# One semaphore per chunk and bank, a query copy on another engine, and an epsilon folded into the square root, in a decode attention and SwiGLU kernel

## The chip, the cores and the metric

The kernel runs on one core of one Trainium2 chip. The metric is the device time of one execution in microseconds. The engines named below are TensorE (PE, with its weight loads as PEld), VectorE (DVE), ScalarE (ACT), GpSimd (POOL) and SyncE (SP, which issues nearly all DMAs). A row that ends in q, such as SPq, stands for the engine's sequencer, the part that reads instructions and hands them to the engine.

## The reference

One token for each of 4 batch rows is normalised, and the sum of an attention block and a feed-forward block is added to it. The attention reads a window of W = 4096 cached keys and values of each of 8 key/value heads, which 4 query heads share.

```python
xn = _layernorm(x, axis=-1)                       # x: (4, 1, 512), eps = 1e-5
# attention: 32 query heads, 8 key/value heads, Dh = 128, W = 4096
q = (xn @ wq) per head
k = k_cache[:, :, Sk - W:, :]; v = v_cache[:, :, Sk - W:, :]    # bfloat16
p = softmax(einsum(q, k) * Dh ** -0.5)
a = einsum(p, v) @ wo
# feed-forward, F = 1792
b = (silu(xn @ w_gate) * (xn @ w_up)) @ w_down
return x + a + b
```

## The kernel before

It is written by hand, engine by engine: each engine has its own program in the order of the code, and semaphores tie them. Nothing is reordered by a scheduler.

SP (`on_sync`) issues the loads on one queue: the weights for the queries, the gate and the up projection, then for each of 8 key/value heads ("groups") 4 MB of keys into one of two buffers `KB` and 4 MB of values into one of two buffers `VB`, then the down projection and the output projection `WO`, whose five pieces (`WOS`) go into the freed key buffer 0. A key load waits until the transposes of two groups earlier are done (`s_tr[15]`), a value load until the products of two groups earlier are done (`s_pv`).

Before the loop, DVE works out mean and variance of the rows (L305 to L309), ACT takes the square root (L275), DVE normalises, PE makes queries, gate and up. DVE stores the queries of all groups in `QT` and those of the first group in `QC` (L317 to L321).

PE then runs a loop of 4 rounds with two groups each (`u` = 0, 1). A group has 128 tiles of keys, handled in 16 chunks `c` of 8 tiles:

- PE transposes a chunk into PSUM (L417) and increments `s_tr[c]`; DVE (11 chunks, L328) or ACT (5 chunks, `ACT_CH`, L280) copies it to `KT`, and PE multiplies it by the queries `QC` (L432) two chunks later. Four chunks fill one PSUM bank `q` of scores.
- DVE takes maxima of each bank (L334), of all (L336), then copies the next group's queries to `QC` (L337); PE transposes the maxima (L439), DVE makes the shift `CM` (L339 to L343), PE adds it to the scores (L444, one matmul for each bank).
- ACT takes the exponentials bank by bank (L283) and PE multiplies them by the values (L453) and sums them (L459), which ends with `s_pv`.
- ACT copies the product to `Osb` (L286, `s_os`), DVE sums the denominators (L346, `s_dn`); PE picks the heads apart in the next group's chunk 2 (`fin`, L466 and L469), and DVE divides (`norm`, L350 to L355).

`spin` (L475) are matmuls without a use for their result. After the loop PE runs `fin` once more, the down projection, a permutation of the heads (L530), and the output projection (L479, L483), each piece when its `WO` load has landed. DVE and ACT copy the result (L373, L299), and ACT issues the store (L301).

A wait compares a semaphore with a number. In the loop that number depends on the round, `r * NB + (q + 1)` for `s_p` for example, since one semaphore `s_p` counts all banks of all groups, `s_ev` all chunks of DVE, `s_ea` all chunks of ACT, and `s_mk` all shifted banks. Each engine's sequencer works such a number out in a register, by an instruction of its own, ahead of the wait.

Of the kernel before, what the change touches and what calls it, by code (L numbers as in the profile page):

```python
# [10 lines left out]
def bass_parallel_sum__sliding_block_cached__swiglu_ffn__decode_kernel(  # L11
# [29 lines left out]
    NB = 4  # L41
# [35 lines left out]
    st_var = sb("st_var", [B, 1], FP32)  # L77
# [82 lines left out]
    s_ev = sem("s_ev")  # L160
    s_ea = sem("s_ea")
# [4 lines left out]
    s_mk = sem("s_mk")  # L166
    s_p = sem("s_p")
# [24 lines left out]
    def on_gpsimd(eng):  # L192
        eng.memset(ident[:], 0.0)
        eng.memset(I4[:], 0.0)
        eng.memset(ones[:], 1.0)
# [73 lines left out]
    def on_scalar(eng):  # L269
# [5 lines left out]
        eng.activation(st_std[:], st_var[:], ACT.Sqrt).then_inc(s_std, 1)  # L275

        def group(r):
            for n, c in enumerate(ACT_CH):
                eng.wait_ge(s_tr[c], r + 1)
                eng.activation(KT[:, c % 4], kt_ps[c % 3], ACT.Copy).then_inc(s_ea, 1)  # L280
            for q in range(NB):
                eng.wait_ge(s_mk, r * NB + (q + 1))
# [3 lines left out]
            eng.activation(Osb[:], O_ps, ACT.Copy).then_inc(s_os, 1)  # L286
# [3 lines left out]
        with eng.Fori(0, HKV) as r:  # L290
            group(r)
# [11 lines left out]
    def on_vector(eng):  # L303
# [3 lines left out]
        eng.bn_aggr(st_mv[:], st_bn[:])  # L307
        eng.drain()
        eng.tensor_scalar(st_var[:], st_mv[:, 1:2], EPS, None, ALU.add).then_inc(s_var, 1)  # L309
# [9 lines left out]
        eng.drain()  # L319

        eng.tensor_copy(QC[:], QT[:, 0])  # L321


        def group(n):
            for c in range(NCH):
                if c not in ACT_CH:
                    eng.wait_ge(s_tr[c], n)
                    eng.tensor_copy(KT[:, c % 4], kt_ps[c % 3]).then_inc(s_ev, 1)  # L328
# [8 lines left out]
            eng.tensor_copy(QC[:], QT[:, bass.ds(n, 1)].rearrange("p o n -> p (o n)"))  # L337
# [37 lines left out]
    def on_tensor(eng):  # L375
# [27 lines left out]
        eng.sem_inc(s_p, NB)  # L403
# [4 lines left out]
        def transposes(r, u, c):  # L408
            if c == 0:
                eng.wait_ge(d_k[u], (r - u) * 8 + 16)  # L410
            if u and c == NCH // 2:
                with eng.If(r > HKV - 2):
                    eng.wait_ge(d_kh, 16)
            if c == 2:
                eng.wait_ge(s_dn, r + 1)
# [4 lines left out]
        def scores(r, c):  # L420
            q = c * CH // BT
            if c % (NCH // NB) == 0:
                eng.wait_ge(s_p, r * NB + (q + 1))
                if q == 3:
                    eng.wait_ge(s_nrm, r + 1)
            if c in ACT_CH:
                eng.wait_ge(s_ea, r * len(ACT_CH) + (ACT_CH.index(c) + 1))
            else:
                eng.wait_ge(s_ev, r * (NCH - len(ACT_CH)) + (c + 1 - sum(a < c for a in ACT_CH)))
# [7 lines left out]
        def maxima(r):  # L437
            eng.wait_ge(s_m, r + 1)
            eng.transpose(mT_ps, m16[:], ident[:]).then_inc(s_mt, 1)  # L439

        def shift(r):
            eng.wait_ge(s_cm, r + 1)
            for q in range(NB):
                mm(ps_S[q][:].rearrange("p (t n) -> p t n", n=NH), own[:],  # L444
                   CM[:].unsqueeze(1).to_broadcast([128, BT, NH]),
                   start=False, stop=True, skip_group_check=True).then_inc(s_mk, 1)

        def pv(r, u):
            for t in range(0, NT, 2):
                n = t // 2 % 4  # L450
                if t % BT == 0:
                    eng.wait_ge(s_p, r * NB + (NB + t // BT + 1))
# [11 lines left out]
        def fin(r):  # L464
            eng.wait_ge(s_dn, r + 1)
            mm(D2_ps, head[:], dsum[:], start=True, stop=True, skip_group_check=True)  # L466
            eng.wait_ge(s_os, r + 1)
# [28 lines left out]
        def warm(r, u, n, k=2):  # L496

            if u:
                spin(n, k)
            else:  # L500
                with eng.If(r > 0):
                    spin(n, k)

        with eng.Fori(0, HKV, 2) as r0:
            for u in range(2):
                r = r0 + u
                for c in range(NCH):
                    transposes(r, u, c)
                    if c == 2:
                        fin(r)  # L510
                    if c >= 2:
                        scores(r, c - 2)
                scores(r, NCH - 2)
                scores(r, NCH - 1)
# [69 lines left out]
```

## Time and profile before

| what | value |
|---|---|
| time, median of 3 runs | 195.59 us (195.41 to 195.85) |
| profiled execution, time | 195.47 us |
| profiled execution, span from its first to its last instruction | 194.2 us |
| TensorE busy | 161.7 us, 83% of the span |
| VectorE busy | 99.7 us, 51% |
| ScalarE busy | 68.1 us, 35% |
| bytes moved by DMA | 81.17 MB, mean 418 GB/s |

The page of the profile lists the busy time of each engine, the span in 40 slices, the DMA queues, the chain of work that ended last and the costliest groups of instructions. A group of rows gives the line of the kernel, the engine, the operation, the tiles written and read, the count, the busy time, the mean duration of one, and the idle time of the engine before it with what ended it. Instructions that only set registers, branch or wait are not counted as busy; the view of one line of the source shows them, as PEldq, ACTq or DVEq.

### The profile page before, as it was taken

The page shows a single profiled execution, that of the slowest core. Times are in us where ns is not written, and L with a number is a line of the kernel's source. Part 1 is how long each engine was busy: PE and PEld are TensorE (multiplying, and loading weights), DVE is VectorE, ACT ScalarE, POOL GpSimd, SP SyncE. Part 2 cuts the span into 40 slices and gives each one's busy share as a digit, 9 for nine tenths or more (in the row PEclk, how much of TensorE's full clock was granted, in tenths as well). Part 3 has the DMA queues.
Part 4 walks back from the last instruction along what each step waited for, and adds up shares of the span by engine and source line. Part 5 has one row for each costly group of instructions (what it writes and reads, how often), then busy time and mean ns, then how long its engine had stood idle before and what let it go on. Part 6 is the DMA issues. An engine that isn't in the chain of part 4 may idle for free.

```text
span 194.2 us, 7150 instructions
## 1 busy us (share of the span) xinstructions
PE 161.7 (83%) x3179; PEld 132.8 (68%) x3179; DVE 99.7 (51%) x209; ACT 68.1 (35%) x92; POOL 5.7 (3%) x32
## 2 busy tenths in 40 slices
PE   0038972986898699999999899989996999999984
PEld 0038973985498649966994798469845984996532
DVE  0210012768177537871886389337933793688120
ACT  5520000352436242625451455315531543362520
POOL 7300000000000000000000000000000000000000
PEclk9999999999699999999999999999999999999999
DMA  6999999999999999999999999999999999999992
GB/s 216 433 437 431 423 429 432 445 429 435 425 435 442 432 422 429 425 439 432 439 432 432 432 432 432 432 439 445 432 439 439 432 398 432 466 432 392 437 407 107
DMA packets 3802, 81.17 MB, mean 418 GB/s; under 512 B 440, under 2 KB 576, under 8 KB 832
## 3 DMA queue, kind: packets, MB, share of 16 engines
q1 hardware_dynamic: 3776, 81.00, 97.3%
q8 instruction: 9, 0.15, 0.3%
q10 hardware_dynamic: 16, 0.01, 0.0%
q14 instruction: 1, 0.01, 0.0%
HBM read 81.01 MB, written 0.00 MB: 417 GB/s over the span
## 4 chain that ended last, share of the span: by engine, by line
DMA 59%; PE 34%; DVE 3%; issue 2%; SPq 1%; DVEq 0%
DMA kbuf<-in_A_k_cache_dram 43%; PE ps_kt L417 19%; DMA kbuf<-in_A_wo_dram 16%; PE ps_s L432 6%; PE ps_o L453 2%; PE ps_s L444 1%; PE ps_s L469 1%; DVE kT L328 1%; PE ps_kt L475 1%; DVE mx L334 1%; PE ps_s L483 1%; PE ps_s L466 1%; SPq L254 0%; PE ps_kt L459 0%; PE ps_kt L439 0%
## 5 line engine op out<-in xcount | busy, mean ns | idle before, releaser
L417 PE MATMUL ps_kt<-ident,kbuf 128*128 128x128 bf16 x1024 | 76.8, 221 | 10.7 <-DMA kbuf<-in_A_k_cache_dram 7.9
L417 PEld LDWEIGHTS ps_kt<-ident,kbuf 128*128 128x128 bf16 x1024 | 59.2, 98 | 13.1 <-DMA kbuf<-in_A_k_cache_dram 9.0
L328 DVE COPY kT<-ps_kt 128x1024 bf16<-128x1024 bf16 x88 | 57.6, 686 | 19.2 <-PE ps_kt L417 17.9
L280 ACT ACTIVATE kT<-ps_kt 128x1024 bf16<-128x1024 bf16 x40 | 40.9, 1023 | 53.0 <-PE ps_kt L417 53.0
L432 PE MATMUL ps_s<-qC,kT 128*128 128x16 bf16 x1024 | 44.7, 170 | 2.6 <-DVE kT L328 1.9
L432 PEld LDWEIGHTS ps_s<-qC,kT 128*128 128x128 bf16 x1024 | 37.4, 97 | 4.2 <-DVE kT L328 4.1
L283 ACT ACTIVATE p<-ps_s 128x512 bf16<-128x512 f32 x32 | 16.5, 603 | 34.0 <-PE ps_s L444 34.0
L334 DVE TENSOR_REDUCE mx<-ps_s 128x16 f32<-128x512 f32 x32 | 22.0, 689 | 5.9 <-PE ps_s L432 3.8
L475 PE MATMUL ps_kt<-own,ones 128*128 128x512 bf16 x82 | 20.7, 380 | 0.0
L453 PE MATMUL ps_o<-vbuf,p 128*32 128x256 bf16 x512 | 18.6, 284 | 0.3
L453 PEld LDWEIGHTS ps_o<-vbuf,p 128*32 128x32 bf16 x512 | 14.6, 100 | 6.0 <-ACT p L283 4.6
L346 DVE TENSOR_REDUCE dsum<-ps_kt 128x16 f32<-128x256 f32 x8 | 3.4, 425 | 28.6 <-PE ps_kt L459 28.6
L459 PE MATMUL ps_kt<-p,ones 128*32 128x256 bf16 x64 | 16.4, 282 | 0.0
L475 PEld LDWEIGHTS ps_kt<-own,ones 128*128 128x128 bf16 x82 | 6.6, 97 | 7.0 <-issue 1.1
L444 PE MATMUL ps_s<-cm,own 128*128 128x512 bf16 x32 | 8.9, 402 | 1.0 <-DVE cm L343 1.0
L380 PE MATMUL ps_s<-i,xn 4*128 4x4 f32 x4 | 0.6, 255 | 10.3 <-DVE xn L313 10.3
L380 PEld LDWEIGHTS ps_s<-i,xn 4*128 4x128 f32 x4 | 0.6, 208 | 10.3 <-issue 10.3
L459 PEld LDWEIGHTS ps_kt<-p,ones 128*32 128x32 bf16 x64 | 6.5, 101 | 0.1
L289 ACT ACTIVATE ex<-ps_o 128x84 f32<-128x84 f32 x1 | 0.2, 240 | 17.4 <-PE ps_o L399 17.4
L444 PEld LDWEIGHTS ps_s<-cm,own 128*128 128x128 bf16 x32 | 2.5, 99 | 5.5 <-DVE cm L343 3.4
L286 ACT ACTIVATE osb<-ps_o 128x256 f32<-128x256 f32 x8 | 3.1, 383 | 8.2 <-PE ps_kt L459 8.2
L359 DVE TENSOR_SCALAR ex<-ex 128x84 f32<-128x84 f32 x1 | 0.2, 204 | 10.9 <-ACT ex L289 10.9
(83 smaller groups left out, 89.8 us busy)
## 6 DMA issues: line engine op xcount, KB each, us to landing
vbuf<-in_A_v_cache_dram SPq DMA_DIRECT2D x8, 4096.0 KB, 30.2
kbuf<-in_A_k_cache_dram SPq DMA_DIRECT2D x7, 4096.0 KB, 26.7
vbuf<-in_A_wq_dram SPq DMA_DIRECT2D x1, 4096.0 KB, 12.4
kbuf<-in_A_k_cache_dram SPq DMA_DIRECT2D x2, 2048.0 KB, 25.4
kbuf<-in_A_wo_dram SPq DMA_DIRECT2D x1, 2048.0 KB, 27.2
wg_sb<-in_B_w_gate_dram SPq DMA_DIRECT2D x1, 1792.0 KB, 16.2
wu_sb<-in_B_w_up_dram SPq DMA_DIRECT2D x1, 1792.0 KB, 21.1
wd_sb<-in_B_w_down_dram SPq DMA_DIRECT2D x1, 1664.0 KB
```

The costliest lines, as they stand in the source:

```text
L280: eng.activation(KT[:, c % 4], kt_ps[c % 3], ACT.Copy).then_inc(s_ea, 1)
L283: eng.activation(P[:, BT * q:BT * (q + 1), :], ps_S[q][:].rearrange("p (t n) -> p t n", n=NH), ACT.Exp, scale=SCALE).then_inc(s_p, 1)
L286: eng.activation(Osb[:], O_ps, ACT.Copy).then_inc(s_os, 1)
L328: eng.tensor_copy(KT[:, c % 4], kt_ps[c % 3]).then_inc(s_ev, 1)
L334: eng.tensor_reduce(mx[:, q, :], ps_S[q][:].rearrange("p (t n) -> p n t", n=NH), AX.X, ALU.max)
L346: eng.tensor_reduce(dsum[:], den_ps.rearrange("p (t n) -> p n t", n=NH), AX.X, ALU.add).then_inc(s_dn, 1)
L417: last = eng.transpose(kt_ps[c % 3][:, k, :], KB[u][:, CH * c + k, :], ident[:])
L432: last = mm(ps_S[q][:, NH * t:NH * (t + 1)], KT[:, c % 4, k, :], QC[:], start=(t == 0), stop=False, skip_group_check=True)
L444: mm(ps_S[q][:].rearrange("p (t n) -> p t n", n=NH), own[:], CM[:].unsqueeze(1).to_broadcast([128, BT, NH]), start=False, stop=True, skip_ ...
L453: mm(O_ps[32 * n:32 * n + 32, :], P[:, t:t + 2, :].rearrange("p t n -> p (t n)"), VB[u][:, t:t + 2, :].rearrange("p t d -> p (t d)"), star ...
L459: last = mm(den_ps[32 * n:32 * n + 32, :], ones[:, 0:32], P[:, DT * e:DT * (e + 1), :].rearrange("p t n -> p (t n)"), start=(e < 4), stop= ...
L475: mm(ps_kt[k][:], ones[:], own[:].unsqueeze(1).to_broadcast([128, 4, 128]), skip_group_check=True)
```

## The change

Three things are changed.

1. The semaphores `s_ev` and `s_ea` become 16 semaphores `s_ev[c]`, one for each chunk; `s_mk` and `s_p` become four each, one for each bank. Each is incremented once in a group, so that every wait in the loop compares with the loop's own counter, which now runs from 1. PE works out three numbers in a round with `snap` (`d` for the loads, `n`, `n1`), and no other.
2. The copy of the next group's queries to `QC` moves from DVE (after the maxima) to ACT (after the copy to `Osb`); `s_os` is incremented by it, and no longer by the copy to `Osb`. The first group's queries are copied to `QC` by DVE from PSUM, where before they were copied from `QT` after a drain.
3. The addition of epsilon on DVE, and the drain ahead of it, go; ACT's square root adds epsilon as its bias, read from a small tile `st_eps` that POOL fills.

```diff
-    s_ev = sem("s_ev")
-    s_ea = sem("s_ea")
+    s_ev = [sem("s_ev%d" % i) for i in range(NCH)]
-    s_mk = sem("s_mk")
-    s_p = sem("s_p")
+    s_mk = [sem("s_mk%d" % i) for i in range(NB)]
+    s_p = [sem("s_p%d" % i) for i in range(NB)]
...
         eng.memset(I4[:], 0.0)
+        eng.memset(st_eps[:], EPS)
...
-        eng.activation(st_std[:], st_var[:], ACT.Sqrt).then_inc(s_std, 1)
+        eng.activation(st_std[:], st_mv[:, 1:2], ACT.Sqrt, bias=st_eps[:, 0:1]).then_inc(s_std, 1)
...
             for q in range(NB):
-                eng.wait_ge(s_mk, r * NB + (q + 1))
+                eng.wait_ge(s_mk[q], n)
                 eng.activation(P[:, BT * q:BT * (q + 1), :], ps_S[q][:].rearrange("p (t n) -> p t n", n=NH),
-                               ACT.Exp, scale=SCALE).then_inc(s_p, 1)
-            eng.wait_ge(s_pv, r + 1)
-            eng.activation(Osb[:], O_ps, ACT.Copy).then_inc(s_os, 1)
+                               ACT.Exp, scale=SCALE).then_inc(s_p[q], 1)
+            eng.wait_ge(s_pv, n)
+            eng.activation(Osb[:], O_ps, ACT.Copy)
+            eng.activation(QC[:], QT[:, bass.ds(n, 1)].rearrange("p o n -> p (o n)"), ACT.Copy).then_inc(s_os, 1)
...
-        eng.bn_aggr(st_mv[:], st_bn[:])
-        eng.drain()
-        eng.tensor_scalar(st_var[:], st_mv[:, 1:2], EPS, None, ALU.add).then_inc(s_var, 1)
+        eng.bn_aggr(st_mv[:], st_bn[:]).then_inc(s_var, 1)
...
-        eng.drain()
-
-        eng.tensor_copy(QC[:], QT[:, 0])
+        eng.tensor_copy(QC[:].rearrange("p (b h) -> p b h", b=B),
+                        q_ps.rearrange("p (k h b) -> p k b h", k=HKV, b=B)[:, 0])
...
             eng.tensor_reduce(m16[:], mx[:].rearrange("p q n -> p n q"), AX.X, ALU.max).then_inc(s_m, 1)
-            eng.tensor_copy(QC[:], QT[:, bass.ds(n, 1)].rearrange("p o n -> p (o n)"))
             eng.wait_ge(s_mt, n)
...
-        def scores(r, c):
+        def scores(c, n):
             q = c * CH // BT
             if c % (NCH // NB) == 0:
-                eng.wait_ge(s_p, r * NB + (q + 1))
+                eng.wait_ge(s_p[q], n)
                 if q == 3:
-                    eng.wait_ge(s_nrm, r + 1)
-            if c in ACT_CH:
-                eng.wait_ge(s_ea, r * len(ACT_CH) + (ACT_CH.index(c) + 1))
-            else:
-                eng.wait_ge(s_ev, r * (NCH - len(ACT_CH)) + (c + 1 - sum(a < c for a in ACT_CH)))
+                    eng.wait_ge(s_nrm, n)
+            eng.wait_ge(s_ev[c], n)
...
-                    eng.wait_ge(s_p, r * NB + (NB + t // BT + 1))
+                    eng.wait_ge(s_p[t // BT], n1)
...
-        with eng.Fori(0, HKV, 2) as r0:
+        with eng.Fori(1, HKV + 1, 2) as m:
+
+            d = eng.snap((m - 1) * 8 + 16)
             for u in range(2):
-                r = r0 + u
+                n = m if u == 0 else eng.snap(m + 1)
+                n1 = eng.snap(n + 1)
```

The first place is TensorE's program in the loop, chunks 6 and 7 of a group's transposes with the scores of chunks 4 and 5 (`qC` and `kT` are the queries and the copied chunk). Before:

```order
L417 MATMUL ps_kt<-ident,kbuf 128x128 x8
L423 REGISTER_ALU
L429 REGISTER_ALU [waits s_p]
L432 MATMUL ps_s<-qC,kT 128x16 [waits s_ev]
L432 MATMUL ps_s<-qC,kT 128x16 x7
L417 MATMUL ps_kt<-ident,kbuf 128x128 x8
L427 REGISTER_ALU
L432 MATMUL ps_s<-qC,kT 128x16 [waits s_ea]
L432 MATMUL ps_s<-qC,kT 128x16 x7
```

The same place with the change:

```order
L415 MATMUL ps_kt<-ident,kbuf 128x128 x8
L427 MATMUL ps_s<-qC,kT 128x16 [waits s_ev4,s_p1]
L427 MATMUL ps_s<-qC,kT 128x16 x7
L415 MATMUL ps_kt<-ident,kbuf 128x128 x8
L427 MATMUL ps_s<-qC,kT 128x16 [waits s_ev5]
L427 MATMUL ps_s<-qC,kT 128x16 x7
```

The instructions that work out a number are gone; the matmuls stand as they stood. TensorE's whole program has 249 such rows before and 201 with the change.

The second place is ScalarE's program from its last chunk copy to the end. The piece of the difference, with the rows of before marked - and those of the change marked +:

```order
-L282 ISA
-L283 ACTIVATE p<-ps_s 128x512 [waits s_mk]
-L282 REGISTER_ALU
-L283 ACTIVATE p<-ps_s 128x512 [waits s_mk]
-L282 REGISTER_ALU
...
 L286 ACTIVATE osb<-ps_o 128x256 [waits s_pv]
-L290 REGISTER_ALU
-L290 COMPARE_AND_BRANCH
...
+L287 ISA
+L287 ACTIVATE qC<-qT 128x16
+L291 REGISTER_ALU
+L291 COMPARE_AND_BRANCH
```

The numbers for `s_mk` go, and one instruction for the address of the queries and the copy to `qC` come in behind the copy to `osb`. ScalarE's program has 32 rows before and 29 with the change.

The third place is VectorE's program from the maxima of the last bank to the end of the loop and the first rows behind it. Before:

```order
L334 TENSOR_REDUCE mx<-ps_s 128x16 [waits s_sc3]
L336 TENSOR_REDUCE m<-mx 128x16
L337 REGISTER_ALU
L337 COPY qC<-qT 128x16
L339 TENSOR_TENSOR junk<-ps_kt,moff 16x128 [waits s_mt]
...
L346 TENSOR_REDUCE dsum<-ps_kt 128x16 [waits s_pv]
L366 REGISTER_ALU
L366 COMPARE_AND_BRANCH
L350 RECIPROCAL den<-ps_s 128x16 [waits s_fin]
```

With the change:

```order
L332 TENSOR_REDUCE mx<-ps_s 128x16 [waits s_sc3]
L334 TENSOR_REDUCE m<-mx 128x16
L336 TENSOR_TENSOR junk<-ps_kt,moff 16x128 [waits s_mt]
...
L343 TENSOR_REDUCE dsum<-ps_kt 128x16 [waits s_pv]
L363 REGISTER_ALU
L363 COMPARE_AND_BRANCH
L347 RECIPROCAL den<-ps_s 128x16 [waits s_fin]
```

Two instructions leave the loop. VectorE's program has 46 such rows before and 43 with the change, and the diff takes two drains besides, which these rows do not show: five instructions fewer in all. SyncE's program is the same in both; GpSimd's has one more, the fill of `st_eps`.

More of the change, by code (lines that the diff above doesn't have):

```diff
@@ L402, in on_tensor @@
         last.then_inc(s_gu, 1)
[L403 removed]
+        for q in range(NB):
+            eng.sem_inc(s_p[q], 1)
         eng.sem_inc(s_dn, 1)
```

82 lines of the change are left out of this document (41 added, 41 removed).

## The prediction

> **What bounds the kernel now.** I read the page first, for the share of each engine, the DMA queues and the chain that ended last.
>
> ```profile
> span 194.2 us, 7150 instructions
> ...
> PE 161.7 (83%) x3179; PEld 132.8 (68%) x3179; DVE 99.7 (51%) x209; ACT 68.1 (35%) x92; POOL 5.7 (3%) x32
> ...
> POOL 7300000000000000000000000000000000000000
> ...
> q1 hardware_dynamic: 3776, 81.00, 97.3%
> q8 instruction: 9, 0.15, 0.3%
> q14 instruction: 1, 0.01, 0.0%
> ...
> DMA 59%; PE 34%; DVE 3%; issue 2%; SPq 1%; DVEq 0%
> ```
>
> No engine is full, but SP's queue q1 keeps the 16 DMA engines busy for 97.3% of the span. The DMA view for the stretch from 78 to 189 us tells whether anything is lost there.
>
> ```profile
> q1 hardware_dynamic: 2170, 47.76, 99.9%
> ```
>
> Nothing is: for 111 us the data queue alone takes 99.9% of the engines. So the loads are a stream that does not break, and only its start and its end can move the time. The waits and the chain of waits show how TensorE stands to it.
>
> ```profile
> PEld ps_kt L417 <- DMA kbuf<-in_A_k_cache_dram: 9.0, 4, 4.6
> SPq L241 <- PE ps_kt L417: 71.8, 5, 28.3
> SPq L267 <- DMA out_dram<-y_sb: 32.3, 1, 32.3
> 159.24 0.34 SPq L254
> 160.09 31.06 DMA kbuf<-in_A_wo_dram
> 191.20 1.23 PE ps_s L483 x16
> 192.44 0.41 DVE y_sb L373
> ```
>
> TensorE waits for keys four times, 9.0 us in all, so it is ahead of the stream. SP does wait for TensorE (71.8 us), but only to queue loads behind others: the output projection is issued at 159.24 and lands some 31 us later, because that much is queued before it. The chain ends with these loads, 1.2 us of matmuls, a copy and the store. The timeline from 183.65 us shows how close TensorE runs behind the stream there.
>
> ```profile
> 183.65 0.38 ACT L286 ACTIVATE osb<-ps_o 128x256 f32<-128x256 f32 x1 [0.83 <-PE ps_kt L459]
> 184.34 0.53 PEld L469 LDWEIGHTS ps_s<-sel,osb 128*128 128x128 f32 x4
> 185.01 0.26 DVE L350 RECIPROCAL den<-ps_s 128x16 f32<-128x16 f32 x1 [0.93 <-PE ps_s L469]
> 186.18 0.45 ACT L294 ACTIVATE oP<-ps_kt 128x64 bf16<-128x64 f32 x1 [2.14 <-PE ps_kt L530]
> 191.20 1.21 PE L483 MATMUL ps_s<-kbuf,oP 128*4 128x256 bf16 x16 [0.63 <-DMA kbuf<-in_A_wo_dram]
> 191.81 0.09 PEld L483 LDWEIGHTS ps_s<-kbuf,oP 128*4 128x4 bf16 x4 [0.20 <-DMA kbuf<-in_A_wo_dram]
> 192.12 0.08 PEld L483 LDWEIGHTS ps_s<-kbuf,oP 128*4 128x4 bf16 x2 [0.22 <-DMA kbuf<-in_A_wo_dram]
> ```
>
> TensorE had done all it could at 190.57 (191.20 less 0.63), waited for the third piece of `WO`, and waited again for the two behind it, for the last till 192.12. Its lead is 0.63 us. Last comes the DMA view for 189.6 to 193 us, whose row gives the rate in 40 slices of 0.085 us.
>
> ```profile
> GB/s 229 386 253 193 350 301 265 289 277 253 349 241 277 229 241 217 145 96 24 24 24 24 24 24 0 0 0 0 0 0 0 0 0 0 0 0 0 0 0 0
> ```
>
> All 16 engines together moved about 430 GB/s (47.76 MB in 111 us), so one moves 27. The six slices at 24, from 191.13 to 191.64, are one engine working alone for 0.5 us while fifteen have nothing left. TensorE's last weight load starts 0.48 us behind its end. That lone engine is what ends the kernel.
>
> Why is it late? The view for 189 to 190 us has one packet that is not data:
>
> ```profile
> q14 instruction: 1, 0.01, 1.9%
> ```
>
> It is 8 KB of an engine's program, and it held one DMA engine for 1.9% of 16 us, 0.30 us, in the last 2 us of the stream. That it held the very engine that is late is an inference from the place and the size (0.30 us in service, and the turn of the data behind it); no view names the engine of a packet.
>
> **The change part by part.** First the registers, by the views of their lines:
>
> ```profile
> L429 PEldq ALU_OP  x80: 32/32/36, 35.9 to 177.0; - x80
> L423 PEldq ALU_OP  x24: 32/32/32, 38.1 to 175.2; - x24
> L427 PEldq ALU_OP  x32: 32/32/32, 38.6 to 175.8; - x32
> L452 PEldq ALU_OP  x32: 32/32/36, 49.3 to 182.5; - x32
> L282 ACTq ALU_OP  x24: 35/35/44, 49.7 to 181.2; - x24
> ```
>
> On TensorE 168 of 32 ns, less the 8 of L452 that stay, are 160 x 32 ns = 5.1 us of its sequencer, 0.64 us in each of 8 groups. Between zero (the sequencer runs ahead of the matmuls) and 0.64 us a group I take about zero for the time, at either end: what TensorE gains in a group it loses at the next wait for keys (9.0 us in four waits), and a lead at the end that grows from 0.63 us does not bring the loads. Without that cover it would be 5.1 us. On ScalarE 24 x 35 ns stand between exponentials and go the same way. The waits themselves stay, and what is queued behind each stays too.
>
> The copy of the queries, by the views of the lines that are nearest in kind:
>
> ```profile
> L337 DVE COPY qC<-qT x8: 159/161/164, 47.9 to 178.9; 128x16 bf16 x8
> L275 ACT ACTIVATE st_std<-st_var x1: 202/202/202, 9.2 to 9.2; 4x1 f32<-4x1 f32 x1
> L289 ACT ACTIVATE ex<-ps_o 128x84 f32<-128x84 f32 x1 | 0.2, 240 | 17.4 <-PE ps_o L399 17.4
> DVE junk L339 <- PE ps_kt L439: 1.9, 8, 0.2
> ```
>
> VectorE loses 161 ns behind the maxima; there it waits for the transposed maxima anyway (L339, 1.9 us over 8 times), so nothing is gained. ScalarE gains one of 161 to 240 ns; I take 0.2, since the smallest activation of this trace is 202. Behind it waits `s_os`, and behind that TensorE's `fin`. In the loop 24 transposes stand ahead of `fin`; the weakest cover is the last `fin`: `Osb` ends at 184.03 (183.65 + 0.38), the copy then at 184.23 to 184.27, and L469 loads at 184.34. The margin is 0.1 us; if handing over costs more than that, the excess, at most 0.2 us by these rows, comes off TensorE's lead of 0.63. Cost zero. The next chunk that ScalarE copies is `c` = 3 of the next group, behind `fin`, so it is not held.
>
> Epsilon and the first queries, by one row and one wait:
>
> ```profile
> L309 DVE TENSOR_SCALAR st_var<-st_mv x1: 142/142/142, 9.0 to 9.0; 4x1 f32<-4x1 f32 x1
> PE ps_s L387 <- DMA vbuf<-in_A_wq_dram: 2.4, 1, 2.4
> ```
>
> VectorE saves 142 ns and two drains; a bias on the square root costs ScalarE between nothing and its own 202 ns again. TensorE waits 2.4 us for the query weights afterwards, so either sign is covered: zero. The fill of `st_eps` delays the load of `x` by one more small memset, under the same 2.4 us.
>
> By instructions, then, the sum is zero. What is left is the code itself. The packet on q14 comes when five engines' programs are at their ends: SP has stood in its last wait for 32.3 us, GpSimd's row in the page is empty after its second slice, TensorE's code comes on q8; VectorE and ScalarE have just left their loops (L350 at 185.01, L294 at 186.18) and read code that they have not read before. One of the two crosses the end of a block of its program there. VectorE's program becomes five instructions shorter and ScalarE's a few, ahead of that place, so the crossing moves that far towards the end or behind it, and the packet may be asked for only when the loads are done. Then the lone engine ends with the others: 0.5 us earlier, at 191.13 in place of 191.64, and the last piece is seen at 191.6 in place of 192.12. TensorE is free by then: from 190.57, its 16 matmuls take 1.21 us less two waits, about 0.8, until 191.4. The gain is 0.5 us; its bounds are 0 (the packet stays, or hit another engine) and 1.0 us (the last 0.40 MB spread evenly over all engines):
>
> ```profile
> DMA packets 263, 0.40 MB, mean 118 GB/s; under 512 B 40, under 2 KB 147, under 8 KB 263
> ```
>
> 0.40 MB at 430 GB/s are 0.93 us from 189.6, so the loads would end at 190.5 and TensorE's own 191.4 would decide, in place of 192.41 (191.20 + 1.21).
>
> The Trainium skill speaks against this term: its page "Runtime: NRT & Kernel Launch", section "Instruction fetch mechanics", has the sequencer fetch the next block while it executes the current one and calls the cost of a crossing mostly hidden. By that the sum is zero, 195.6 us. It names 16 KiB blocks; q8's 9 packets of 0.15 MB agree, q14's 8 KB does not. The same section has a taken branch outside a window of two blocks fetch again; TensorE's loop branches back three times, and the row for 78 to 189 us lists no q8 packet, so here it does not.
>
> The profiled execution took 195.47 us, 1.3 more than its span and 0.12 less than the median of 195.59. Less 0.5 it is 194.97, as a median 195.1.
>
> **The rivals.** *Nothing that lasts* (195.6 us). The packet is still asked for before 189 us, because the block ends earlier in the program than I think, or ScalarE's, where only few instructions go, is the one; or the late engine was another. For it: every instruction term is zero. A measurement of this kernel tells about 0.2%, 0.4 us, from no change.
>
> *A block of code lands worse* (slower). The row for 76 to 78 us is one TensorE block:
>
> ```profile
> q8 instruction: 1, 0.02, 2.9%
> ```
>
> It holds one DMA engine for 2.9% of 32 us, 0.93 us. TensorE's blocks are now cut at other instructions. If one more falls to an engine that is already late, that engine ends 0.9 us later still: 195.6 + 0.9 = 196.5 us. It decides as soon as the engine ends over 0.4 us behind 191.64. Against it: TensorE's program gets shorter, so there should be no more blocks.
>
> *ScalarE's copy holds the end* (slower). The price is 0.2 us of `fin`, and it decides only beyond the lead of 0.63 us: 195.6 unless TensorE also loses 0.8 us somewhere, then 196.0.
>
> *TensorE's registers are on the path* (faster): 195.6 - 5.1 = 190.5 us. The 99.9% row excludes it, since no byte less is moved.
>
> **How the numbers follow.** Lone engine gone: 0.50, 195.1 us, by itself 194.8 to 195.3. Nothing that lasts: 0.38, 195.4 to 195.8. A block lands worse: 0.08. ScalarE's copy: 0.03. Registers: 0.01. The range of 194.8 to 195.8 holds the first two and leaves out 0.12. Faster by over 0.2%: the first and the last, 0.51; within: 0.38; slower: 0.11.
>
> **What would show it.** Right: no q14 packet in the last us of the stream, no slices at the rate of one engine at its end, no idle time of 0.6 us before L483, and a span about 0.5 us shorter with q1 still at 97%. Also TensorE waiting longer for keys, VectorE's L339 as before, and L469 where it was. Wrong: the lone engine is there without a q14 packet, or the packet is there and no engine is late; or a q1 share that falls below 97%, which would mean that something starves the stream.

## The result, and the profile after

The changed kernel takes 195.18 us (median of 13 runs, 195.01 to 195.38) against 195.67 us for the kernel before, measured beside it (13 runs, 195.41 to 196.46). The ratio is 0.997, with a 95% interval of 0.9959 to 0.9981: 0.49 us faster by the medians. Forecast were 195.1 us and a gain of 0.5 us.

The page of the changed kernel, the rows that answer to those of before:

```profile
span 193.9 us, 6951 instructions
...
PE 163.8 (84%) x3179; PEld 135.2 (70%) x3179; DVE 99.0 (51%) x200; ACT 69.1 (36%) x100; POOL 5.7 (3%) x33
...
q1 hardware_dynamic: 3776, 81.00, 97.5%
q8 instruction: 8, 0.13, 0.2%
q10 hardware_dynamic: 16, 0.01, 0.0%
...
PE 48%; DMA 44%; DVE 5%; issue 1%; SPq 1%; ACT 0%; DVEq 0%
```

There are 199 instructions fewer (7150 less 6951), and SP's loads fill 97.5% of the engines' time, 97.3% before: the bound is the same. The row of q14 is missing. The ninth packet of q8 is gone too, but that says nothing: before, it came at 193.4 us, behind the loads, and two variants below whose TensorE program is as long as the one of before also show eight. The chain now has more of TensorE (48%, was 34%) and less of DMA (44%, was 59%); the rows of the end tell why. First the DMA view of the changed kernel for 189.6 to 193 us, 40 slices of 0.085 us:

```profile
GB/s 277 277 386 193 289 277 301 265 325 265 289 277 289 265 277 205 121 72 48 24 24 24 12 0 0 0 0 0 0 0 0 0 0 0 0 0 0 0 0 0
DMA packets 255, 0.41 MB, mean 120 GB/s; under 512 B 38, under 2 KB 138, under 8 KB 255
```

Six slices at the rate of one engine have become three and a half, some 0.3 us in place of 0.5. Then the timeline of the changed kernel, from ScalarE's copies to the end:

```profile
184.16 0.38 ACT L286 ACTIVATE osb<-ps_o 128x256 f32<-128x256 f32 x1 [0.84 <-PE ps_kt L454]
184.44 0.21 ACT L287 ACTIVATE qC<-qT 128x16 bf16 x1
...
184.86 0.53 PEld L464 LDWEIGHTS ps_s<-sel,osb 128*128 128x128 f32 x4
...
189.61 0.60 PE L478 MATMUL ps_s<-s,sel 128*4 128x256 f32 x4 [0.70 <-ACT s L298]
...
190.04 2.08 PE L478 MATMUL ps_s<-kbuf,oP 128*4 128x256 bf16 x32
191.51 0.09 PEld L478 LDWEIGHTS ps_s<-kbuf,oP 128*4 128x4 bf16 x4 [0.18 <-DMA kbuf<-in_A_wo_dram]
191.85 0.08 PEld L478 LDWEIGHTS ps_s<-kbuf,oP 128*4 128x4 bf16 x2 [0.25 <-DMA kbuf<-in_A_wo_dram]
...
192.17 0.41 DVE L370 CAST y_sb<-ps_s 4x256 bf16<-4x256 f32 x1 [5.04 <-PE ps_s L478]
```

L478 is before's L483. Its matmuls of 32 tiles now run in one stretch of 2.08 us from 190.04: the wait of 0.63 us for the third piece of `WO` is gone. The copy of the queries (L287) takes 0.21 us, and the weight load of `fin` (L464) follows the end of `Osb` by 0.32 us (184.86 less 184.54), before by 0.31 (184.34 less 184.03): at the end of the kernel the copy costs nothing. The last piece is seen at 191.85, 0.27 us earlier than in the profile before.

So this profile shows only 0.3 us. Two things account for it. The profiled executions lie on opposite sides of their medians, 195.30 us against 195.18 with the change and 195.47 against 195.67 before. And TensorE was itself later here: the matmuls of `s` (189.61) began 0.52 us later than before:

```profile
189.09 0.60 PE L483 MATMUL ps_s<-s,sel 128*4 128x256 f32 x4 [0.70 <-ACT s L297]
```

The lead of 0.63 us was used up. That is why the chain now runs back through TensorE instead of stopping at the load of `WO`.

Whether TensorE gained in its groups by the numbers it no longer works out is seen at the first transposes of the last two groups. The chain of waits of the changed kernel has the first of them and its timeline the second:

```profile
149.01 1.51 PE ps_kt L415 x24
```

```profile
166.44 0.73 PE L415 MATMUL ps_kt<-ident,kbuf 128*128 128x128 bf16 x10
```

The group between them takes 17.43 us. The same two views of the kernel before:

```profile
148.65 1.51 PE ps_kt L417 x24
```

```profile
166.00 0.79 PE L417 MATMUL ps_kt<-ident,kbuf 128*128 128x128 bf16 x11
```

There it is 17.35 us. This group did not get shorter, and it began 0.36 us later, when its keys had landed. The waits of the changed kernel, for keys and for the transposed maxima:

```profile
PEld ps_kt L415 <- DMA kbuf<-in_A_k_cache_dram: 9.6, 4, 4.6
DVE junk L336 <- PE ps_kt L434: 2.5, 8, 0.3
```

TensorE waits 9.6 us for keys, again four times, where it was 9.0: of the 5.1 us that 160 numbers less could spare it, little is seen here, and that is waited away. (By the trace it is 168 rows ALU_OP and 24 FUSED_REGOPS less, some 6.3 us, with 27 instructions on semaphores more; the prediction's sum left out the FUSED_REGOPS.) VectorE's wait (L336, before L339) rose from 1.9 to 2.5 us: part of the 1.3 us of the eight copies that left it (8 x 161 ns) is now waiting.

### The profile page after: what moved, and what is told of

Its sections match the earlier page's. It is cut to its first block, busy times and chain, and to the rows that moved or that the text cites. A ratio compares the mean times of both kernels' runs of the same rounds, so it can differ in the third digit from the quotient of the medians.

```text
span 193.9 us, 6951 instructions
## 1 busy us (share of the span) xinstructions
PE 163.8 (84%) x3179; PEld 135.2 (70%) x3179; DVE 99.0 (51%) x200; ACT 69.1 (36%) x100; POOL 5.7 (3%) x33
## 3 DMA queue, kind: packets, MB, share of 16 engines
q1 hardware_dynamic: 3776, 81.00, 97.5%
## 4 chain that ended last, share of the span: by engine, by line
PE 48%; DMA 44%; DVE 5%; issue 1%; SPq 1%; ACT 0%; DVEq 0%
DMA kbuf<-in_A_k_cache_dram 44%; PE ps_kt L415 23%; PE ps_s L427 8%; PE ps_o L448 5%; PE ps_kt L470 4%; DVE kT L326 2%; PE ps_s L439 2%; PE ps_s L464 2%; DVE mx L332 2%; PE ps_s L478 1%; PE ps_s L474 1%; PE ps_s L461 1%; PE ps_kt L454 1%; PE ps_kt L434 0%; ACT s L298 0%
## 5 line engine op out<-in xcount | busy, mean ns | idle before, releaser
L415 PE MATMUL ps_kt<-ident,kbuf 128*128 128x128 bf16 x1024 | 78.2, 224 | 9.0 <-DMA kbuf<-in_A_k_cache_dram 8.5
L415 PEld LDWEIGHTS ps_kt<-ident,kbuf 128*128 128x128 bf16 x1024 | 60.6, 100 | 11.2 <-DMA kbuf<-in_A_k_cache_dram 9.6
L427 PEld LDWEIGHTS ps_s<-qC,kT 128*128 128x128 bf16 x1024 | 38.4, 97 | 4.6 <-DVE kT L326 4.1
L448 PE MATMUL ps_o<-vbuf,p 128*32 128x256 bf16 x512 | 19.1, 289 | 0.3
L454 PE MATMUL ps_kt<-p,ones 128*32 128x256 bf16 x64 | 16.9, 287 | 0.0
L439 PE MATMUL ps_s<-cm,own 128*128 128x512 bf16 x32 | 8.3, 380 | 1.0 <-DVE cm L340 1.0
L464 PE MATMUL ps_s<-sel,osb 128*128 128x16 f32 x36 | 5.8, 275 | 0.0
```

Of the source, the lines that this page charges most:

```text
L415: last = eng.transpose(kt_ps[c % 3][:, k, :], KB[u][:, CH * c + k, :], ident[:])
L427: last = mm(ps_S[q][:, NH * t:NH * (t + 1)], KT[:, c % 4, k, :], QC[:], start=(t == 0), stop=False, skip_group_check=True)
L439: mm(ps_S[q][:].rearrange("p (t n) -> p t n", n=NH), own[:], CM[:].unsqueeze(1).to_broadcast([128, BT, NH]), start=False, stop=True, skip_ ...
L448: mm(O_ps[32 * n:32 * n + 32, :], P[:, t:t + 2, :].rearrange("p t n -> p (t n)"), VB[u][:, t:t + 2, :].rearrange("p t d -> p (t d)"), star ...
L454: last = mm(den_ps[32 * n:32 * n + 32, :], ones[:, 0:32], P[:, DT * e:DT * (e + 1), :].rearrange("p t n -> p (t n)"), start=(e < 4), stop= ...
L464: last = mm(O2_ps, Osb[:, Dh * h:Dh * (h + 1)], sel[:, NH * h:NH * (h + 1)], start=(h == 0), stop=(h == 1), skip_group_check=True)
```

## The experiments

A word that recurs: the **length** of an engine's program, that is every instruction that it holds, waits and drains too. Before, VectorE has 64, ScalarE 35 and TensorE 2256; with the change 59, 33 and 2217. A drain is an instruction without work of its own, which I use to make a program longer.

**The two halves of the change.** The first keeps the new semaphores and undoes the rest (VectorE again 64 long, ScalarE 31):

```diff
-        eng.activation(st_std[:], st_mv[:, 1:2], ACT.Sqrt, bias=st_eps[:, 0:1]).then_inc(s_std, 1)
+        eng.activation(st_std[:], st_var[:], ACT.Sqrt).then_inc(s_std, 1)
...
-            eng.activation(Osb[:], O_ps, ACT.Copy)
-            eng.activation(QC[:], QT[:, bass.ds(n, 1)].rearrange("p o n -> p (o n)"), ACT.Copy).then_inc(s_os, 1)
+            eng.activation(Osb[:], O_ps, ACT.Copy).then_inc(s_os, 1)
...
+            eng.tensor_copy(QC[:], QT[:, bass.ds(n, 1)].rearrange("p o n -> p (o n)"))
```

> The semaphores alone: the query copy and the epsilon are as before, so VectorE's program has all of its instructions again (64, the change has 59), TensorE's is short (2217 for 2256) and ScalarE's shorter than both (31 for 35). Theory: the block of VectorE's program is what the end of the loads waits for, so the q14 packet is back in the last 2 us of the loads and the time is that of before, 195.6 us. Rival, ScalarE's block: no packet, 195.2. Rival, TensorE's registers and waits: 195.2, packet or not.

Measured: 195.56 us (195.42 to 195.82), ratio 0.9981 (0.9965 to 0.9998); the kernel before took 195.73 beside it. Its DMA view for 189 to 190 us has the packet,

```profile
q14 instruction: 1, 0.01, 1.9%
```

and from 189.6 us, in slices of 0.085 us:

```profile
GB/s 361 277 434 60 458 193 301 193 325 265 265 277 253 349 241 277 205 217 157 96 36 24 24 24 24 24 24 0 0 0 0 0 0 0 0 0 0 0 0 0
```

The packet and six slices of a lone engine are back. Its waits for keys:

```profile
PEld ps_kt L417 <- DMA kbuf<-in_A_k_cache_dram: 12.3, 6, 4.7
```

They are 3.3 us longer than before, and 0.6 us in the changed kernel's profile: some of what TensorE is spared it waits, and none of it brings the loads.

The second half is the kernel before with the copy on ScalarE and epsilon as the bias, and the old semaphores (VectorE 59, ScalarE 37, TensorE 2256):

```diff
-        eng.activation(st_std[:], st_var[:], ACT.Sqrt).then_inc(s_std, 1)
+        eng.activation(st_std[:], st_mv[:, 1:2], ACT.Sqrt, bias=st_eps[:, 0:1]).then_inc(s_std, 1)
...
-            eng.activation(Osb[:], O_ps, ACT.Copy).then_inc(s_os, 1)
+            eng.activation(Osb[:], O_ps, ACT.Copy)
+            eng.activation(QC[:], QT[:, bass.ds(r + 1, 1)].rearrange("p o n -> p (o n)"), ACT.Copy).then_inc(s_os, 1)
...
-            eng.tensor_copy(QC[:], QT[:, bass.ds(n, 1)].rearrange("p o n -> p (o n)"))
```

> The other half: the query copy on ScalarE and the epsilon as bias, with the semaphores and register sums of before. VectorE's program is as short as with the change (59), TensorE's as long as before (2256), ScalarE's longer than both (37). Theory: no q14 packet, 195.2 us. Rival, ScalarE's block: the packet is there and the time 195.6. Rival, TensorE's registers and waits: 195.6 without a packet.

Measured: 195.22 us (195.12 to 195.76), ratio 0.9971 (0.9956 to 0.9985). Its DMA view for 189.6 to 193 us:

```profile
GB/s 410 265 422 169 374 181 337 265 265 289 337 289 265 277 301 241 169 157 84 48 24 0 0 0 0 0 0 0 0 0 0 0 0 0 0 0 0 0 0 0
```

and the last piece in its timeline:

```profile
191.71 0.08 PEld L481 LDWEIGHTS ps_s<-kbuf,oP 128*4 128x4 bf16 x2 [0.24 <-DMA kbuf<-in_A_wo_dram]
```

No q14 packet, one slice of a lone engine, and the last piece at 191.71, where the profile before has 192.12. So this half alone brings 0.51 us, as much as the whole change. The register instructions that the first half saves bring at most the 0.2 us between it and the kernel before, and the spans below say that they bring nothing.

**The packet alone.** The changed kernel, with drains on VectorE ahead of its loop and nothing else. Five make VectorE 64 long again, three make it 62:

```diff
+        for _ in range(5):
+            eng.drain()
```

> The whole change, with five empty drains on VectorE ahead of its loop, which make its program as long as before (64) and do nothing else. Theory: the q14 packet is back and the time is 195.6 us. Both rivals: 195.2 and no packet.

Measured with five: 195.59 us (195.28 to 195.82), ratio 0.9981 (0.9966 to 0.9996). Its DMA view for 189 to 190 us has

```profile
q14 instruction: 1, 0.01, 1.9%
```

and from 189.6 us, in slices of 0.085 us:

```profile
GB/s 253 325 289 145 530 96 362 217 241 313 265 265 289 253 265 265 229 193 72 72 36 24 24 24 24 24 0 0 0 0 0 0 0 0 0 0 0 0 0 0
```

Five useless instructions, which VectorE passes before its loop, take 0.41 of the 0.49 us away again (195.59 less 195.18, measured at different times), and the packet and the lone engine are back.

> The whole change, with three empty drains on VectorE ahead of its loop in place of five: 62 instructions, between the change's 59 and the 64 of before. It narrows down where the block ends. Theory: either the packet is in the last 2 us of the loads and the time is 195.6 us, or it is not and the time is 195.2; nothing between.

Measured with three: 194.95 us (194.86 to 195.09), ratio 0.9955 (0.9938 to 0.9971); the kernel before took 195.62 beside it. Its DMA view for 194 to 195 us, behind the end of the span at 193.7, has the packet, at 194.55 us:

```profile
q14 instruction: 1, 0.01, 1.9%
```

The view from 189.6 us shows no lone engine but for half a slice:

```profile
GB/s 313 458 253 398 181 362 301 241 325 289 277 301 265 253 253 181 145 84 72 48 12 0 0 0 0 0 0 0 0 0 0 0 0 0 0 0 0 0 0 0
```

Three drains cost nothing, two more cost 0.64 us (by medians measured at different times). It is not the drains' time, but the length of the program: between 62 and 64 instructions VectorE asks for another block while the loads still run.

**Late or only there?** If the packet costs because it comes late, then asking for it early should cost nothing. The kernel before, with 14 drains on VectorE ahead of its loop (length 78), so that the end of the block falls into the loop:

```diff
+        for _ in range(14):
+            eng.drain()
```

> The kernel before, with 14 empty drains on VectorE ahead of its loop, so that the place at which the block is asked for moves from behind the loop into it and is passed in the first round. Theory: the q14 packet comes before 60 us; what it costs there is open: 195.2 us if its DMA engine is one that has time to spare at the end, 195.6 or more if it is one that is late anyway. Both rivals: the packet stays at the end, 195.6.

Measured: 195.56 us (195.34 to 195.99), ratio 0.9975 (0.9957 to 0.9993). Its DMA view for 53 to 54 us has the packet, at 53.5 us,

```profile
q14 instruction: 1, 0.01, 1.9%
```

and yet the end, from 189.6 us, looks like this:

```profile
GB/s 386 313 241 361 205 277 265 277 325 289 373 253 289 265 277 265 253 193 133 72 36 24 24 24 12 0 0 0 0 0 0 0 0 0 0 0 0 0 0 0
```

The lone engine stays for 0.3 us, no more than in the changed kernel's profile; but this profiled execution, 195.35 us, is the second fastest of its twelve, and the median is 0.34 us above that of the second half of the change, measured beside it (195.22). So the early block costs about as much as the late one. The expectation had left that open.

**What the spans say.** Each run also has its span, from the first to the last instruction of the program. It leaves out the 1.2 to 1.5 us of the time that most runs have outside of it, and it separates the kernels better than the time does:

| kernel | VectorE's length | its further block at | span, median of the runs | time less span, median |
|---|---|---|---|---|
| before (94 runs beside the variants) | 64 | 189.3 us | 194.3 us | 1.27 to 1.30 us |
| new semaphores alone | 64 | 189.5 us | 194.3 us | 1.26 us |
| change and 5 drains | 64 | 189.6 us | 194.3 us | 1.26 us |
| before and 14 drains | 78 | 53.5 us | 194.3 us | 1.24 us |
| change and 3 drains | 62 | 194.55 us | 193.7 us | 1.25 us |
| query copy and epsilon alone | 59 | none | 193.8 us | 1.41 us |
| the change | 59 | none | 193.8 us | 1.39 us |

VectorE's block costs 0.5 to 0.6 us of the span, early or late, and the register instructions cost nothing of it. The last column holds something that nobody forecast: the kernels whose VectorE program has 59 instructions take some 0.1 us more outside of the span. That is 0.14 of the 0.23 us by which the kernel with three drains (194.95 us) is faster than the change (195.18); why it is so, no run shows. The kernel before has runs that are long outside of the span, 10 of the 35 beside the two halves by 0.4 us and more, and they raise its median there (195.73 us).

**What the single packets say.** The trace keeps the start, duration and size of every packet. In the kernel before, data packets of one size take the same time after 40 us, within 20 ns (196 ns for 5 KB, 309 ns for 8 KB, 1213 ns for 32 KB), but for those that begin just as a packet of a program ends, and in one place the one behind it as well. These are the data packets behind the blocks of VectorE and ScalarE (whose runs follow below):

| block | took | data packets behind it | in place of | lost by that DMA engine |
|---|---|---|---|---|
| VectorE, late (before, 189.3 us) | 309 ns | 504 and 429 ns (5 KB) | 196 ns each | 0.85 us |
| VectorE, early (14 drains, 53.5 us) | 309 ns | 1744 ns (32 KB) | 1213 ns | 0.84 us |
| ScalarE, late (33 drains, 187.76 us) | 309 ns | 551 ns (8 KB) | 309 ns | 0.55 us |
| ScalarE, early (36 drains, 59.5 us) | 309 ns | 1453 ns (32 KB) | 1213 ns | 0.55 us |

So a block costs its DMA engine more than its own 0.31 us, because the data behind it are held up too. With the new semaphores alone and with 5 drains the packets behind VectorE's block take 504 and 429, and 501 and 429 ns, and from there one follows the other without a gap to the very last packet of the stream: the lone engine is the one that served the block. Why the data are held up, and why more behind VectorE's block than behind ScalarE's, no run shows.

**The other engine.** ScalarE's program made longer in the changed kernel, by 31, 33 and 36 drains (length 64, 66 and 69):

```diff
+        for _ in range(31):   # 33, 36
+            eng.drain()
```

> The whole change, with 31 empty drains on ScalarE ahead of its loop, which bring its program from 33 instructions to 64, the length at which VectorE's asks for its next block; VectorE's stays at 59. Theory: a block is a block, so a q14 packet comes again, now for ScalarE, and if ScalarE crosses the same place behind its loop, it comes in the last us of the loads and the time is 195.6 us. Rival, only VectorE's program matters: no packet, 195.2.

> The whole change, with 33 empty drains on ScalarE ahead of its loop. With 31 its block was asked for after its 64th and last instruction, the store; with 36, in the loop. So the place is the 65th instruction, and with 33 that is the copy of the result behind the loop, which ScalarE's sequencer reads at about 184 us. Theory, the place of the crossing in time is what costs, whoever crosses: the q14 packet comes between 185 and 191.5 us and the time is 195.6 us. Rival, only VectorE's blocks cost: 195.2.

> The whole change, with 36 empty drains on ScalarE ahead of its loop in place of 31 (its program has 69 instructions, VectorE's 59). With 31 the q14 packet came at 193.7 us, when ScalarE issued its last instruction, the store, and cost nothing. Five more put the same place in the program ahead of the store, behind the loop. Theory, the place of the crossing in time is what costs: the q14 packet comes between 184 and 191.5 us and the time is 195.6 us. Rival, only VectorE's blocks cost: 195.2.

Measured:

| drains | length | packet at | median (range) | ratio (95%) | before, beside it |
|---|---|---|---|---|---|
| 31 | 64 | 193.66 us | 195.12 (194.96 to 195.42) | 0.9974 (0.9962 to 0.9987) | 195.60 |
| 33 | 66 | 187.76 us | 195.37 (195.26 to 195.52) | 0.9976 (0.9965 to 0.9988) | 195.75 |
| 36 | 69 | 59.5 us | 195.30 (195.09 to 195.68) | 0.9973 (0.9956 to 0.9990) | 195.62 |

With 31 the packet comes, as expected, but behind the store, and costs nothing; 195.6 us was expected. With 36 it was meant for the end and fell into the loop, so that run says only what an early packet costs. With 33 it came in the last 4 us of the stream, and the loss that I expected did not follow. That kernel's DMA view for 187 to 188 us has

```profile
q14 instruction: 1, 0.01, 1.9%
```

and from 189.6 us, in slices of 0.085 us:

```profile
GB/s 410 410 205 374 253 301 169 301 289 265 362 289 301 277 241 229 205 145 97 36 24 12 0 0 0 0 0 0 0 0 0 0 0 0 0 0 0 0 0 0
```

The same packet with the same 0.30 us of service, and one slice and a half of a lone engine. Against the run with 31 drains it is 0.25 us, against the changed kernel 0.19, and the ratios to the kernel before do not differ. The medians of the spans are 193.7, 194.0 and 193.9 us for 31, 33 and 36 drains: ScalarE's block costs 0.1 to 0.3 us, VectorE's 0.5 to 0.6. The table of the packets has the reason for most of that: ScalarE's takes 0.55 us from its DMA engine, VectorE's 0.85, and some 0.3 us of either go unnoticed. With 33 drains, too, the data behind the block run without a gap to the last packet of the stream.

**How bad a TensorE block is.** First try: 256 increments of an unused semaphore at TensorE's start, to shift where its blocks end.

```diff
+        s_pad = sem("s_pad")
+        for _ in range(256):
+            eng.sem_inc(s_pad, 1)
```

> The whole change, with 256 increments of an unused semaphore at the start of TensorE's program, where it waits 10 us for the normalised rows anyway: one q8 block of 16 KB more (9 in place of 8) while the loads run. This prices the rival of the prediction in which one more block falls to an engine. If the ninth block falls to an engine that has none, it costs nothing that lasts beyond the others: 195.2 us. If it falls to one that is late anyway: 0.9 us or more on top, 196.1 or more.

Measured: 215.41 us (212.72 to 215.59), ratio 1.101 (1.0993 to 1.1027). This tests nothing of what it was made for, as three views of that kernel show. Its timeline has TensorE's first matmul at 40 us,

```profile
40.37 0.61 PE L380 MATMUL ps_s<-i,xn 4*128 4x4 f32 x4 [40.37 <-issue]
```

its waits have SP's queue behind TensorE's first results,

```profile
SPq L251 <- PE ps_s L387: 40.7, 1, 40.7
```

and its page has the data queue:

```profile
q1 hardware_dynamic: 3776, 81.00, 89.5%
```

TensorE started at 40 us, since 256 increments held it until then, 0.16 us each. SP waited for its first results before it could issue a load of values into the buffer of the query weights, the stream broke, and q1 fell to 89.5%. It does show the other side of the bound: the gap in the stream was not made good, and the kernel takes 20 us longer.

The second try puts 62 small matmuls without use ahead of TensorE's loop, which moves its blocks without delaying anything that the loads need:

```diff
+        for _ in range(62):
+            mm(ps_kt[2][:, 0:NH], ones[:], own[:, 0:NH], skip_group_check=True)
```

> The whole change, with 62 small matmuls without use on TensorE ahead of its loop, where it waits about 5 us for the first keys. They cost 62 x 23 ns = 1.4 us there and lengthen its program by 124 instructions, so that TensorE crosses the end of one of its own blocks behind the loop and not at the very end: a ninth q8 packet of 16 KB comes between 185 and 191 us. It prices the prediction's rival of a block that lands worse. Theory: it holds a DMA engine for 0.93 us and the data behind it longer; 195.2 us if that engine is one that is done early, up to 196.6 if it is late anyway. Rival, small matmuls and no block: 195.2 with the packet missing.

Measured: 196.58 us (196.40 to 196.98), ratio 1.004 (1.0023 to 1.0057). Its DMA view for 190 to 192 us has a block of TensorE's program,

```profile
q8 instruction: 1, 0.02, 3.0%
```

the view from 189.6 us the end of the stream,

```profile
GB/s 217 434 229 398 241 265 253 410 289 253 337 253 265 241 205 133 145 109 109 48 0 24 0 24 0 0 24 24 24 24 24 24 24 24 24 0 0 0 0 0
```

and the timeline TensorE's wait:

```profile
192.26 1.05 PE L480 MATMUL ps_s<-kbuf,oP 128*4 128x256 bf16 x16 [1.42 <-DMA kbuf<-in_A_wo_dram]
```

The block comes at 190.2 us. For the last 15 slices, 1.3 us, at most one engine moves data, and TensorE stands idle for 1.42 us. It costs 1.4 us against the changed kernel, 1.3 us by the spans (195.1 against 193.8). By the single packets the block took 0.97 us, and the four data packets behind it 227, 225, 225 and 132 ns in place of 84: some 1.4 us lost by one DMA engine, whose packets then run without a gap to the last of the stream.

**An attempt to beat both.** If single engines are what ends the kernel, the last loads should lie on more of them. The rows of the down projection `WDX` go out by two DMAs of 8 partitions in place of four of 4:

```diff
-        for o in range(4):
-            eng.dma_start(WDX[o:JX:4], wdx_ap[o]).then_inc(d_wd, 16)
+        for o in range(2):
+            eng.dma_start(WDX[o:JX:2], wdx_ap[o]).then_inc(d_wd, 16)
```

> The whole change, with the small rest of the down projection (16 partitions) loaded by two DMAs of 8 partitions in place of four of 4, so that by the Trainium skill's page on DMA it runs on 8 engines in place of 4, with half as much on each. If the late block of code falls among the four engines, their load is why it cannot be absorbed; here, without a late block, the time should stay at 195.2 us, and rise towards 195.8 if the second four engines are ones that blocks of TensorE's code made late.

Measured: 196.36 us (196.26 to 196.40), ratio 1.004 (1.0027 to 1.0054), 1.2 us above the changed kernel, where 195.2 to 195.8 was expected. Its end, from 189.6 us:

```profile
GB/s 542 265 374 373 386 470 398 422 373 446 374 349 470 277 289 325 229 277 145 169 253 169 181 181 193 193 121 108 72 48 36 24 24 24 0 0 0 0 0 0
```

From about 191.1 to 191.8 us the rate is 145 to 253 GB/s, that of some 5 to 9 engines: now several have too much left. But most of the loss is older. At 189.6 us this kernel still has 0.73 MB to load and the changed one 0.41, and up to 180 us both had loaded some 76.7 MB. Between 180 and 185 us the small rows of `WDX` are loaded, by the order of the issues (the 4.2 MB of `WO` follow them). The DMA view of that stretch with two DMAs of 8 partitions, and then of the changed kernel:

```profile
q1 hardware_dynamic: 143, 1.84, 100.4%
```

```profile
q1 hardware_dynamic: 172, 2.18, 101.9%
```

The engines are as busy and move 0.34 MB less, 0.8 us at 430 GB/s. That is where two thirds of the 1.2 us are lost; why less is moved there stays open.

On top of that, the last large piece of `WO` by 16 DMAs of 8 partitions each, to spread it in another way:

```diff
-        for q in range(len(WOS) - 1):
+        for q in range(len(WOS) - 2):
...
+        for p in range(0, 128, 8):
+            eng.dma_start(WO[p:p + 8, WOS[-2]:NR, :], wo_ap[p:p + 8, WOS[-2]:NR, :]).then_inc(d_wo[-1], 16)
```

> As the kernel with two DMAs, and the last piece of the output projection, 128 KB, loaded by 16 DMAs of 8 partitions, so that it runs on the first 8 engines alone and the other 8 have 8 KB less each, 0.3 us at 27 GB/s. If TensorE's code blocks made just the other 8 late, the loads end 0.3 us earlier and the time is 194.9 us, faster than both kernels. If they are mixed among the first 8, these end 0.3 us later: 195.5.

Measured: 199.60 us (199.46 to 199.76), ratio 1.0208 (1.0194 to 1.0222). The timeline:

```profile
161.28 18.02 SPq L268 DMA_DIRECT2D kbuf<-in_A_wo_dram  x16
...
195.98 0.38 PE L480 MATMUL ps_s<-kbuf,oP 128*4 128x256 bf16 x2 [2.79 <-DMA kbuf<-in_A_wo_dram]
```

SP needed 18 us to issue the sixteen, 1.1 us each, and TensorE waited 2.79 us for the last, until 195.98 us. The DMA view shows no data behind 193.4 us, so this wait is not for bytes, and the slow issue was over at 179.3; what it is stays open. Expected were 194.9 or 195.5 us. Neither is a better kernel.

## Why the prediction was right

**The stream bounds, and instructions sum to zero: shown.** The first half of the change takes 160 and more register instructions off TensorE, 5.1 us of its sequencer by the prediction's count, and the span stays at 194.3 us. The rival that would have given 190.5 us is out. The other terms taken at nothing are at nothing: the copy on ScalarE takes 207 ns where 0.2 us was put down, and `fin` follows `Osb` as before (0.32 us, before 0.31), so the margin of 0.1 us that was named as the weakest cover held. (The smallest activation of the trace is 199 ns, not 202; nothing hangs on it.)

**The packet on q14 and the 0.5 us: shown.** The program block of 8 KB at 189.3 us, VectorE's, is what the change removes. It comes and goes with two instructions, and the span with it: 194.3 us in the four kernels that have it while the loads run, 193.7 to 193.8 in the three that do not. The prediction inferred that the block held the engine that is late; the single packets of the two kernels that bring it back show that engine, and that it loses 0.31 us to the block and 0.54 to the slower data behind it. The prediction put down the first part as a number and the second only in words ("the turn of the data behind it").

**What was off, and what was luck.** Of the signs that were named, no q14 packet, the missing wait of 0.63 us and q1 at 97% came. Others did not: slices at the rate of one engine are still there (three and a half), VectorE's wait at L339 rose from 1.9 to 2.5 us, and the first weight load of `fin` came 0.52 us later. A lone engine without a q14 packet was even named as a sign of being wrong. It is not that here, because the span goes with the block in seven kernels, but it shows that the block is not all that makes an engine late: the loads ended at 191.3 to 191.6 us without VectorE's block, not at 191.13. The prediction did not say whether VectorE or ScalarE asks for the block; it is VectorE. It put the last piece at 191.6 in the profile, and it was 191.85, since it took TensorE to be free from 190.57, and in this execution TensorE worked until 191.4 without a wait for loads. The lead of 0.63 us is no fixed quantity: in the profiles with the block the same wait is 0.63, 0.54, 0.46 and 0.30 us. Its wording, that the crossing moves "behind" the loads, made lateness the point, and that is too narrow, since VectorE's block at 53 us costs as much as at 189 us. And that the time gained 0.49 us, so near to 0.5, is in part luck: the span gained 0.5 us, but the change added some 0.1 us outside of the span that the prediction did not have. By these two it would be 0.4 us, near the lower end of the interval of the ratio (0.37 to 0.80 us).

**The slower rival was real, but another kernel's.** A block that lands worse was priced at 0.9 us, from the 0.93 us of a TensorE block, on top of 195.6: 196.5 us. Forced by 62 matmuls it gave 196.58, but that is agreement by chance: the kernel with the matmuls has no block of VectorE's, so the step is 1.4 us from 195.18, half as much again as its price. The change itself shortens TensorE's program, and nothing of the kind happened.

**The page of the Trainium skill.** "Runtime: NRT & Kernel Launch", section "Instruction fetch mechanics", calls the cost of a crossing mostly hidden, which would have left 195.6 us. For the engine that crosses, the runs agree: VectorE waits for TensorE at the end anyway (5.8 us before the last copy). But the block is fetched by a DMA engine that has data to move too, and that is not hidden here: 0.5 to 0.6 us of the span for VectorE's block, 1.3 us for TensorE's.

## What to carry to other kernels

Where one load stream fills all DMA engines, as it does here, a change in instructions can act on the time through the program's own bytes: look for packets of the kind "instruction" while the stream runs, and for slices at the rate of one engine at its end. Count the instructions of the engines that are off the path as well, since two of them can decide whether a block is fetched during the stream; and before work is taken off an engine for its time, ask which wait takes that time back. A pad or a trimmed instruction is then worth a run of its own, because it tells the effect of a change from that of its length.

## What the runs showed of the hardware that was not expected

- A block of an engine's program is loaded by a DMA engine among the data, and the data behind it are held up too. VectorE's 8 KB took 0.31 us, the data behind them 0.53 to 0.54 us longer than others of their size, and the kernel 0.5 to 0.6 us of span, at 53 us as at 189 us. ScalarE's 8 KB held the data up by 0.24 us.
- For VectorE the further block is asked for between 62 and 64 instructions (behind the end of the work with 62, at 189.3 to 189.6 us with 64); for ScalarE between 64 and 66 (193.66 us with 64, 187.76 with 66, in the loop at 59.5 with 69).
- With 59 instructions of VectorE the kernels take 1.38 to 1.42 us outside of their span, with 62, 64 and 78 it is 1.24 to 1.30.
- TensorE needs about 0.16 us for an increment of a semaphore that stands by itself: 256 of them held its first matmul until 40.4 us.
- SP needed 1.1 us for each of 16 DMAs of 8 partitions (18.02 us in all), with loads queued ahead of them.
- Issuing a small load in two DMAs of 8 partitions in place of four of 4 cost 1.2 us, some 0.8 of it between 180 and 185 us, where the engines were as busy and moved 0.34 MB less.
